# A decode attention block: most K and V loads issued by GpSimd as software DMAs, eight rows to a packet

## The chip, the cores and the metric

The kernel runs on one core of one Trainium2 chip. The metric is device time in microseconds for one execution. Three runs of the kernel before gave 1303.33, 1303.16 and 1303.37 us; the median is 1303.33 us. A separate execution was taken by the hardware profiler, and every row shown below comes from it.

## The reference

One decode step for two sequences (B = 2, one new token each, model width D = 512). It normalises x, projects it to one query for each of 32 heads of 128 channels, attends over a cache of 8192 positions, projects back, and then runs a channel MLP of width 1792. All numbers are float32.

```python
q = ((layernorm(x) @ wq).reshape(B, 1, 32, 128)).transpose(0, 2, 1, 3)
scores = einsum("bhqd,bhkd->bhqk", q, k_cache) * 128 ** -0.5
o = einsum("bhqk,bhkd->bhqd", softmax(scores), v_cache)
h = x + o.reshape(B, 1, 4096) @ wo
y = layernorm(layernorm(h))
out = h + gelu(y @ w1 + b1) @ w2 + b2
```

k_cache and v_cache are 2 x 32 x 8192 x 128 floats each: 268 MB each. Everything else together is about 24 MB. Each cache element is used once.

## The kernel before, in words

**Units.** The work is cut into 32 units. Unit i = 2g + b is a pair of heads (2g and 2g + 1) of sequence b. A unit's keys are 8.39 MB, and so are its values. One load puts such a block on 128 partitions, 64 partitions to a head, so that each partition receives one contiguous row of 64 KB: 128 positions of 128 channels. Sixteen DMA engines share the 128 rows, eight rows each.

**Slots.** SBUF has room for three such blocks, the three `kv` slots. `load` (L407) puts keys into slot 0 or 1 in turn (`i % 2`), and values into slot 2. So a load of values can start only when the previous values were used up, and a load of keys only when the keys of two units earlier were. Slot 2 first holds wq; after the last units, slot 0 takes wo and then w1, w2 and the biases, and slot 1 takes the last unit's values. The last values are loaded in two parts of 96 and 32 positions, and the very first keys in two halves.

**One unit.** VectorE multiplies the keys with the query (`multiply`, L441) in two chunks of 80 and 48 positions. GpSimd adds the upper 64 channels of the first chunk's products to the lower 64 (`halve`, L445), one instruction a unit (three in unit 0, which has four chunks of 32). VectorE sums over channels (`add_up`, L449) and takes the maximum (`row_max`, L456). After the second unit of a pair the maximum over partitions, the exponentials on ScalarE (L473) and the sum follow. TensorE multiplies the probabilities of unit i - 2 with its values (`values`, L485) while unit i's keys are worked on.

**The order of issue.** Instructions are written out by hand, and each engine runs its own in the order written. In the loop (L535 to L574), iteration i first issues the load of V[i - 2] (for i = 1 that is V[0], and none at i = 2), then that of K[i + 1], then the multiplies and the `halve` of unit i, then `values(i - 2)`. All these loads are issued by SyncE (SP), and SP has no other work, so its queue holds loads alone. A load waits on SP until its slot is free: for V on TensorE's `values`, for K on VectorE's `row_max`. `Waits` (L36) works out the semaphore waits of every instruction from the areas it reads and writes. `own` names a semaphore of its own for a load, so that it can be counted apart from the 16 shared ones.

**Behind the loop** (L577 on) the order written is: wo (SP, L419); a gather of 64 more rows of it into `wgt`, an indirect DMA of GpSimd's (L420), the one software DMA of the kernel before; V[30] (L578, SP); the head outputs and their projection (`project_all`, which needs wo and `wgt`); `values(30)`; V[31] in its two parts (L586, SP); biases, w1 and w2 (SP), which need the place where wo lay; then 24 matmuls that only keep TensorE's clock up (`keep_warm`), `values(31)`, the output projection's rest and the MLP. TensorE waits for the last piece of w2, adds it up, and the result is stored (L712).

Of the kernel before, what the change touches and what calls it, by code (L numbers as in the profile page):

```python
# [16 lines left out]
SHORT = (32, 32, 32, 32)  # L17
NG = 4
TH = 2
FILL = (24, 1, 4, 2, 3)  # L20
SR = 4
LW = 6
# [13 lines left out]
class Waits:  # L36
# [76 lines left out]
    def place(self, eng, op, areas):  # L113
        areas = [(x, w) for x, w in areas if x is not None]
        queue = (eng,)
        if "DMA" in op:
            kind = "soft" if eng == "Pool" else "hard"
            proc = kind, self.lane.get(kind, 0) % self.LANES
            if kind == "hard" and self.own:
                proc = self.own  # L120
            else:
                self.lane[kind] = self.lane.get(kind, 0) + 1
        else:
            proc = queue
        self.sem(proc)
        need = {}
        if proc != queue and self.count[proc]:
            need[proc] = self.count[proc]
        for (name, parts, cols), writes in areas:
            for r in self.mem.get(name, ()):  # L130
                if not (writes or r[4]) or not (r[2] & parts and r[3] & cols):
                    continue
                if r[0] == proc == queue:
                    if eng == "PE" or eng != "Pool" and not r[4]:
                        continue
                need[r[0]] = max(need.get(r[0], 0), r[1])
        clock = self.clock.setdefault(queue, {})
        todo = []
        for p, t in sorted(need.items(), key=lambda x: -self.after[x[0], x[1]][0]):
            if clock.get(p, 0) >= t:  # L140
                continue
            todo.append((p, t))
            for q, u in self.after[p, t][1].items():
                clock[q] = max(clock.get(q, 0), u)
        tick = self.count[proc] + 1
        if op != "Ldweights":
            self.count[proc] = tick
            self.after[proc, tick] = (len(self.after), {**clock, proc: tick})
        for (name, parts, cols), writes in areas:
            held = self.mem.setdefault(name, [])  # L150
            if writes:
                held[:] = [r for r in held if r[2] & ~parts or r[3] & ~cols]
            else:
                held[:] = [r for r in held if r[4] or r[0] != proc or r[2] & ~parts or r[3] & ~cols]
            held.append((proc, tick, parts, cols, writes))
        return proc, todo[::-1]
# [108 lines left out]
def tile_decode_block(nc, waits, x, k, v, wq, wo, wog, w1, bias, w2, out):  # L265
    B, H, SK, DH = k.shape
# [23 lines left out]
    def slot(at):  # L290
        return kv.tile([P, ROW], F32, name="kv", tag="kv", at=at)
# [22 lines left out]
    nc.gpsimd.memset(lt4, 0.0)  # L314
    oall = const.tile([P, H - TH, B], F32, name="oall")
    og = const.tile([P, SR, B], F32, name="og")
# [90 lines left out]
    def load(src, i, parts):  # L407
        g, b = units[i]
        t = slot(i % 2 if src is k or i == NU - 1 else 2)
        rows = src[b, 2 * g:2 * g + 2].rearrange("h (p j) d -> (h p) (j d)", j=NS2)  # L410
        waits.own = ("v" if src is v else "k", b) if len(parts) == 1 else None
        for s0, n in parts:
            nc.sync.dma_start(t[:, s0 * DH:(s0 + n) * DH], rows[:, s0 * DH:(s0 + n) * DH])
        waits.own = None
        return t

# [68 lines left out]
    def values(i, t):  # L485
        g, b = units[i]
        so, nu, w = so2[g == GL], NS2 // 4, 16
        for u in range(nu):
            n = u % NG
            if i == NU - 1 and u == 0:  # L490
                keep_warm(FILL[0])
            pe.matmul(so[32 * n:32 * n + w], ptz[b][:, u, :], t[:, u * 512:(u + 1) * 512],
# [26 lines left out]
    def project_all(wot):  # L519
        so = so2[0]  # L520
        parts = [(oall[:, h, :], wot[:, h, :]) for h in range(GA)]
        parts += [(og[:, r, :], wgt[:, r, :]) for r in range(SR)]
        parts += [(oall[:, h, :], wot[:, h - 2, :]) for h in range(GA + 2, H - TH)]
        n = len(parts)
# [7 lines left out]
    full = [(0, NS2)]  # L532
    assert NS2 == sum(LONG) == sum(SHORT)
    KT, VT = {0: load(k, 0, [(0, NS2 // 2), (NS2 // 2, NS2 // 2)])}, {}
    for i, (g, b) in enumerate(units):  # L535
        if i == 1 or i >= 3:
            j = max(i - 2, 0)
            VT[j] = load(v, j, full)
        if i + 1 < NU:
            KT[i + 1] = load(k, i + 1, full)  # L540
# [64 lines left out]
    def cut(parts, n):  # L605
        at[0] += n
        return late[:parts, at[0] - n:at[0]]

    zeros = cut(P, (TH + 1) * 32)
    nc.gpsimd.memset(zeros, 0.0)  # L610
    otz = zeros[:, :TH * 32].rearrange("p (s m) -> p s m", s=TH)
    lane = zeros[:B, TH * 32:]
    nc.gpsimd.tensor_copy(lane[:, 0:B], ident[:B, :B])
# [4 lines left out]

    wl = wot[:, H - 2 - TH:, :]
    wsum = const.tile([P, TH], F32, name="wsum")  # L620
# [20 lines left out]
    def keep_warm(n):  # L641
        for _ in range(n):
            pe.matmul(wp, wb[:, :P], wb, start=True, stop=True)
# [9 lines left out]
    def spread(row):  # L653
        return row.rearrange("d (n j c) -> d n c j", n=NG, c=DC)
# [8 lines left out]
    nc.vector.tensor_copy(b1t, b1p)  # L663
    keep_warm(FILL[1])
    for s in range(TH):
        for n in range(NG):
            pe.matmul(pc[32 * n:32 * n + 32], otz[:, s], spread(wlc[:, s])[:, n], start=False, stop=(s == TH - 1))
    keep_warm(FILL[2])
    cen = cut(P, DC * 32)
# [11 lines left out]
    for s in range(TH):  # L681
        for n in range(NG):
            pe.matmul(po2[32 * n:32 * n + 32], otz[:, s], wl[:, s, n * P:(n + 1) * P], start=False, stop=False)
    keep_warm(FILL[3])
    FH = FN // 2
# [10 lines left out]
    nc.scalar.activation(junk[:, 1:2], std, AF.Gelu_apprx_tanh)  # L696
    keep_warm(FILL[4])

# [67 lines left out]
```

## Time and profile before

| What | us |
|---|---|
| median of three runs | 1303.33 |
| the profiled execution, its own time | 1303.13 |
| the profiled execution's span | 1301.3 |
| VectorE busy | 973.6 (75%) |
| TensorE matmul busy | 385.9 (30%) |
| GpSimd busy | 364.6 (28%) |
| DMA queue q1 (SP's loads): share of 16 engines' span | 99.6% |

The span runs from the first to the last instruction of the profile; the execution's own time is 1.8 us longer. In the rows, `SPq` marks a DMA at the time when SP issues it; the transfer itself runs later. `kv<-in_k_dram` is a load of keys, `kv<-in_v_dram` one of values. In a timeline row the columns are start, length, engine, line, operation, tiles, shapes, count, and in brackets the idle time of the engine before it and what ended it. In a row of the chain the columns are start, length and what it was.

### The profile page before, as it was taken

The page shows a single profiled execution, that of the slowest core. Times are in us where ns is not written, and L with a number is a line of the kernel's source. Part 1 is how long each engine was busy: PE and PEld are TensorE (multiplying, and loading weights), DVE is VectorE, ACT ScalarE, POOL GpSimd, SP SyncE. Part 2 cuts the span into 40 slices and gives each one's busy share as a digit, 9 for nine tenths or more (in the row PEclk, how much of TensorE's full clock was granted, in tenths as well). Part 3 has the DMA queues.
Part 4 walks back from the last instruction along what each step waited for, and adds up shares of the span by engine and source line. Part 5 has one row for each costly group of instructions (what it writes and reads, how often), then busy time and mean ns, then how long its engine had stood idle before and what let it go on. Part 6 is the DMA issues. An engine that isn't in the chain of part 4 may idle for free.

```text
span 1301.3 us, 6275 instructions
## 1 busy us (share of the span) xinstructions
PE 385.9 (30%) x2756; PEld 118.2 (9%) x2756; DVE 973.6 (75%) x284; ACT 49.1 (4%) x156; POOL 364.6 (28%) x64
## 2 busy tenths in 40 slices
PE   3002322213332122333203232212323212332369
PEld 0000100101010010101001010000101001010113
DVE  1989989777779777779877778877778977777911
ACT  0000000000000000000000000000000000000011
POOL 1433333311333321233321233331133331133300
PEclk9556665566666556666556666556666556666569
DMA  9999999999999999999999999999999999999998
GB/s 403 435 451 420 447 421 445 425 429 439 423 447 423 445 422 447 423 437 433 425 443 425 443 423 447 421 441 429 433 437 423 445 423 447 421 445 425 438 422 373
DMA packets 10821, 561.13 MB, mean 431 GB/s; under 512 B 1398, under 2 KB 1398, under 8 KB 1660
## 3 DMA queue, kind: packets, MB, share of 16 engines
q1 hardware_dynamic: 10664, 560.48, 99.6%
q0 software_dynamic: 144, 0.52, 0.1%
q8 instruction: 5, 0.08, 0.0%
q14 instruction: 4, 0.03, 0.0%
q10 hardware_dynamic: 4, 0.00, 0.0%
HBM read 561.53 MB, written 0.00 MB: 432 GB/s over the span
## 4 chain that ended last, share of the span: by engine, by line
DMA 57%; DVE 37%; issue 2%; POOL 2%; PE 1%; SPq 0%; POOLq 0%
DMA kv<-in_k_dram 50%; DVE kv L441 22%; DVE s L449 15%; DMA kv<-in_w_dram 3%; POOL kv L445 2%; DMA wgt<-in_wog_dram,gidx 2%; DMA kv<-in_wq_dram 2%; PE so L188 1%; DVE qs L395 0%; DVE oall L507 0%; PE qps L188 0%; DVE rl L482 0%; PE sm L236 0%; SPq L598 0%; DVE q L385 0%
## 5 line engine op out<-in xcount | busy, mean ns | idle before, releaser
L441 DVE TENSOR_TENSOR kv<-kv,qps 128x10240 f32<-128x10240 f32 (+1 forms) x66 | 554.5, 8423 | 206.3 <-DMA kv<-in_k_dram 205.8
L445 POOL TENSOR_TENSOR kv<-kv 128x5120 f32<-128x5120 f32 (+1 forms) x34 | 356.0, 10470 | 864.8 <-DVE kv L441 864.8
L236 PE MATMUL so<-kv,pt 128*16 128x512 f32 x1920 | 273.6, 734 | 708.4 <-DMA kv<-in_v_dram 708.4
L449 DVE TENSOR_REDUCE s<-kv 128x48 f32<-128x6144 f32 (+1 forms) x66 | 381.5, 5820 | 1.4 <-POOL kv L445 0.3
L236 PEld LDWEIGHTS so<-kv,pt 128*16 128x16 f32 x1920 | 57.6, 113 | 901.1 <-DMA kv<-in_v_dram 712.6
L497 ACT ACTIVATE ss<-so 128x512 f32<-128x512 f32 x16 | 9.6, 597 | 1062.1 <-PE so L236 1047.8
L473 ACT ACTIVATE pt<-s,nb 64x128 f32<-64x128 f32 x64 | 25.5, 399 | 141.8 <-DVE nb L468 140.5
L236 PE MATMUL sm<-ident,mx 128*1 128x128 f32 x30 | 8.8, 293 | 57.3 <-DVE mx L456 57.3
L461 DVE TENSOR_REDUCE gm<-sm 1x4 f32<-1x256 f32 x16 | 6.6, 412 | 25.5 <-PE sm L236 25.0
L236 PE MATMUL sm<-sel,ss 128*128 128x4 f32 x120 | 15.8, 255 | 12.1 <-ACT ss L497 12.1
L236 PE MATMUL sm<-lt,ones 128*128 128x4 f32 x30 | 8.8, 365 | 34.9 <-ACT pt L473 34.9
L188 PE MATMUL qps<-kv,pt 128*16 128x512 f32 x128 | 16.7, 683 | 6.1 <-DMA kv<-in_v_dram 6.1
L236 PEld LDWEIGHTS sm<-sel,ss 128*128 128x128 f32 x120 | 14.5, 191 | 25.9 <-ACT ss L497 25.9
L385 DVE COPY q<-so 128x512 f32<-128x512 f32 x1 | 0.7, 691 | 20.8 <-PE so L188 20.8
L626 DVE TENSOR_SCALAR kv<-kv,wmean 128x512 f32<-128x512 f32 x2 | 1.0, 518 | 20.3 <-PE qps L188 20.3
L507 DVE TENSOR_TENSOR kv<-sm,rl 128x4 f32<-128x4 f32 x1 | 0.2, 163 | 19.3 <-PE sm L188 19.3
L188 PE MATMUL qps<-kv 128*32 128x128 f32 (+2 forms) x178 | 13.3, 296 | 0.6 <-DMA kv<-in_w_dram 0.6
L188 PE MATMUL so<-kv,yT 128*4 128x512 f32 x64 | 9.9, 787 | 11.5 <-DMA kv<-in_wq_dram 11.5
L188 PE MATMUL sm<-ident,mx 128*1 128x128 f32 x2 | 0.7, 371 | 40.2 <-DVE mx L456 40.2
L473 ACT ACTIVATION_READ_ACCUMULATOR pt<-s,nb 64x1 f32 x64 | 11.8, 184 | 0.0
L236 PE MATMUL qps<-qs,pick 4*128 4x128 f32 x60 | 11.1, 307 | 0.0
L236 PEld LDWEIGHTS sm<-lt,ones 128*128 128x128 f32 x30 | 7.5, 311 | 36.2 <-ACT pt L473 36.2
(108 smaller groups left out, 119.9 us busy)
## 6 DMA issues: line engine op xcount, KB each, us to landing
kv<-in_k_dram SPq DMA_DIRECT2D x2, 4096.0 KB, 35.7
kv<-in_wo_dram SPq DMA_DIRECT2D x1, 7680.0 KB, 46.3
kv<-in_v_dram SPq DMA_DIRECT2D x1, 6144.0 KB, 42.1
kv<-in_w_dram SPq DMA_DIRECT2D x1, 3584.0 KB, 34.3
kv<-in_v_dram SPq DMA_DIRECT2D x1, 2048.0 KB, 46.5
kv<-in_w_dram SPq DMA_DIRECT2D x1, 1792.0 KB, 38.2
kv<-in_w_dram SPq DMA_DIRECT2D x1, 1024.0 KB, 40.2
kv<-in_w_dram SPq DMA_DIRECT2D x1, 512.0 KB, 41.0
```

The costliest lines, as they stand in the source:

```text
L188: getattr(self.nc.tensor, what)(*aps, **how)
L236: ins = getattr(pe, what)(*aps, **how)
L385: nc.vector.tensor_copy(q2, so2[0])
L441: nc.vector.tensor_tensor(kc, kc, QP[g][:, b, None, :].to_broadcast([P, chunks(i)[c], DH]), op=ALU.mult)
L445: nc.gpsimd.tensor_tensor(kc[:, :, 0:HP], kc[:, :, 0:HP], kc[:, :, HP:DH], op=ALU.add)
L449: nc.vector.tensor_reduce(S[i][:, a:z], chunk(i, c, t)[:, :, 0:n], axis=AX.X, op=ALU.add)
L461: nc.vector.tensor_reduce(gm, MT.pop(g).rearrange("o b (s p) -> o b s p", s=2), axis=AX.X, op=ALU.max, negate=True)
L473: nc.scalar.activation(ptz[b][q, :, 4 * m:4 * m + 4], s[q], AF.Exp, bias=nb[q, b, e:e + 1], scale=SCALE, accum_out=lt4[q, m:m + 1])
L497: nc.scalar.activation(SS[g], so2[g == GL], AF.Copy)
L507: nc.vector.tensor_tensor(to, *(x.rearrange("p (b s) -> p s b", b=B) for x in (OP.pop(g), RL.pop(g))), op=ALU.mult)
L626: nc.vector.tensor_scalar(wlc[:, s], wl[:, s], wmean[:, s:s + 1], None, op0=ALU.subtract)
```

## The change

`load` chooses the issuing engine. Loads made in one part go to GpSimd's queue as software DMAs, except K[0] and K[1]; so do V[0] to V[30] and K[2] to K[31], 61 loads. K[0], K[1] and the two parts of V[31] stay on SP, and so do wq, wo, w1, w2 and the biases. [...] The place of each load in the written order is the same, but it now stands in GpSimd's order, among its `halve` instructions, and not in SP's. Its waits are the same. `own` now holds for software loads too.

```diff
+JOIN = True
 ...
             kind = "soft" if eng == "Pool" else "hard"
             proc = kind, self.lane.get(kind, 0) % self.LANES
-            if kind == "hard" and self.own:
+            if self.own:
                 proc = self.own
 ...
         rows = src[b, 2 * g:2 * g + 2].rearrange("h (p j) d -> (h p) (j d)", j=NS2)
-        waits.own = ("v" if src is v else "k", b) if len(parts) == 1 else None
+        soft = len(parts) == 1 and (src is v or i > 1)
+        queue = nc.gpsimd if soft else nc.sync
+        waits.own = ("v" if src is v else "k", b) if soft else None
         for s0, n in parts:
-            nc.sync.dma_start(t[:, s0 * DH:(s0 + n) * DH], rows[:, s0 * DH:(s0 + n) * DH])
+            queue.dma_start(t[:, s0 * DH:(s0 + n) * DH], rows[:, s0 * DH:(s0 + n) * DH], single_packet=soft and JOIN)
         waits.own = None
```

## The prediction

> **What bounds the kernel now.** I read the page's shares first, then the chain of waits, then the timelines of single engines around three places: the middle, the start and the end.
>
> ```profile
> span 1301.3 us, 6275 instructions
> PE 385.9 (30%) x2756; PEld 118.2 (9%) x2756; DVE 973.6 (75%) x284; ACT 49.1 (4%) x156; POOL 364.6 (28%) x64
> q1 hardware_dynamic: 10664, 560.48, 99.6%
> q0 software_dynamic: 144, 0.52, 0.1%
> ...
> 421.73 47.51 DMA kv<-in_k_dram
> 499.14 47.50 DMA kv<-in_k_dram
> ```
>
> SP's loads keep all 16 DMA engines busy for 99.6% of the span; no other engine comes near. The two chain pieces are the same step one pair of units later: 499.14 - 421.73 = 77.41 us for four loads of 8.39 MB, so 19.35 us a load and 2.42 us for each of the eight 64 KB rows that an engine moves of it. The kernel is a queue of transfers that must never run dry. Any idle time of the DMA engines is added to the end, and nothing but faster transfers can take time away.
>
> **The middle: no cost for the moved issue.** These are the timelines of SP, GpSimd and VectorE over one pair.
>
> ```profile
> 419.87 0.33 SPq L413 DMA_DIRECT2D kv<-in_v_dram  x1
> ...
> 402.75 11.04 POOL L445 TENSOR_TENSOR kv<-kv 128x5120 f32<-128x5120 f32 x1 [27.67 <-DVE kv L441]
> 441.47 11.04 POOL L445 TENSOR_TENSOR kv<-kv 128x5120 f32<-128x5120 f32 x1 [27.68 <-DVE kv L441]
> ...
> 430.56 17.29 DVE L441 TENSOR_TENSOR kv<-kv,qps 128x10240 f32<-128x10240 f32 x2 [8.54 <-DMA kv<-in_k_dram]
> ```
>
> The load of V goes out at 419.87, when `values` has freed slot 2; the load of K follows at 421.73, where the chain's piece begins. At that time the previous K is still in flight: VectorE gets it at 430.56. So V has 10.7 us before the DMA engines run dry. On GpSimd the written order is V, K, `halve`. The earlier `halve` is over at 413.79 and the next has its operand only at 441.4, so GpSimd sits idle where both issues now fall. What is queued behind them there is that next `halve`, and behind it VectorE's sum; both come 20 us later. Issue on GpSimd costs nothing here, as long as a software load is ready within 10.7 us. Taking the waits from SP gains nothing either.
>
> **What a software load needs to get ready.** Before has one software DMA, the gather of `wgt` behind the loop. The first two rows are queue totals between 1190 and 1260 us, the third comes from the table of DMA issues (last number: us to landing), the last two from GpSimd's timeline.
>
> ```profile
> q1 hardware_dynamic: 516, 29.98, 99.0%
> q0 software_dynamic: 144, 0.52, 1.9%
> ...
> wgt<-in_wog_dram,gidx POOLq DMA_INDIRECT x1, 25.3
> ...
> 1215.84 11.04 POOL L445 TENSOR_TENSOR kv<-kv 128x5120 f32<-128x5120 f32 x1 [27.66 <-DVE kv L441]
> 1227.06 1.24 POOL L420 DMA_INDIRECT wgt<-in_wog_dram,gidx  x1 [0.18 <-issue]
> ```
>
> It has 144 packets, nine an engine, of tiny size, yet lands after 25.3 us. That fits two queues taking turns packet by packet: each small packet waits for one large one of SP's. A partition's row of wo is 30 x 512 floats, 60 KB: 2.42 x 60/64 = 2.27 us; nine turns behind rows of 2.27 to 2.42 us are 21.0 us. The rest, 4.3 us, is the estimate from issue to ready, indices included; GpSimd is held 1.24 us of it. The shortest that any row shows is the final store, below, 1.4 us from issue to landing. I take 3 us for a plain load, bounds 1.4 and 4.3.
>
> **The start: one gap.** GpSimd, SP, TensorE, and the chain:
>
> ```profile
> 49.95 4.52 POOL L445 TENSOR_TENSOR kv<-kv 128x2048 f32<-128x2048 f32 x1 [2.25 <-DVE kv L441]
> 110.99 11.03 POOL L445 TENSOR_TENSOR kv<-kv 128x5120 f32<-128x5120 f32 x1 [25.91 <-DVE kv L441]
> 140.75 11.13 POOL L445 TENSOR_TENSOR kv<-kv 128x5120 f32<-128x5120 f32 x1 [18.73 <-DVE kv L441]
> ...
> 105.81 0.33 SPq L413 DMA_DIRECT2D kv<-in_v_dram  x1
> ...
> 140.26 9.15 PE L236 MATMUL so<-kv,pt 128*16 128x512 f32 x64 [9.88 <-DMA kv<-in_v_dram]
> ...
> 62.95 37.12 DMA kv<-in_k_dram
> ```
>
> K[2] lands at 62.95 + 37.12 = 100.07, so K[3] behind it at 119.42, and V[1] must be ready by then. SP issued it at 105.81. On GpSimd it stands behind unit 2's `halve`, which waits for K[2] and its multiply and runs from 110.99 to 122.02. V[1] is ready at 122.02 + 3 = 125.0: the DMA engines idle for **5.6 us** (4.0 to 6.9). Elsewhere the lead holds: V[0] stands behind unit 0's last `halve`, ready at 54.47 + 3 = 57.5, while K[1] occupies the engines until 100.07 - 2 x 19.35 = 61.4 (even 4.3 us fits). V[2] stands behind the `halve` that ends at 151.88, and behind `values(1)`, now over at 125.0 + 19.35 + 9.15 = 153.5; ready at 156.5, before K[4] lands at 163.7. From V[3] on `values` is the later of the two, as in the middle.
>
> **The end: V[30] is overtaken.** TensorE's timeline, SP's, and the issue table:
>
> ```profile
> 1224.30 9.84 PE L236 MATMUL so<-kv,pt 128*16 128x512 f32 x64 [27.58 <-DMA kv<-in_v_dram]
> 1262.21 9.66 PE L188 MATMUL qps<-kv,pt 128*16 128x512 f32 x64 [6.06 <-DMA kv<-in_v_dram]
> 1271.80 5.35 PE L188 MATMUL qps<-kv 128*128 128x512 bf16 x24
> 1277.08 7.06 PE L188 MATMUL qps<-kv,pt 128*16 128x512 f32 x64
> 1297.01 1.08 PE L188 MATMUL qps<-kv 128*32 128x128 f32 x32 [0.43 <-DMA kv<-in_w_dram]
> 1298.26 1.07 PE L188 MATMUL qps<-kv 128*32 128x128 f32 x24 [0.17 <-DMA kv<-in_w_dram]
> ...
> 1196.11 0.33 SPq L419 DMA_DIRECT2D kv<-in_wo_dram  x1
> 1234.29 1.28 SPq L413 DMA_DIRECT2D kv<-in_v_dram  x3
> ...
> out_dram<-kv SPq DMA_DIRECT2D x1, 4.0 KB, 1.4
> ```
>
> In SP's one queue the order was K[31], V[29], wo, V[30], V[31] in two parts, w1, w2. Now wo and V[31] are in SP's queue, and K[31], V[29], the gather, V[30] in GpSimd's. [...] V[30], behind the gather in its queue, starts after about four rows of V[31]'s first part, each 2.42 x 48/64 = 1.81 us: **7.2 us** late (three to five rows: 5.4 to 9.1). [...]
>
> Behind V[30] TensorE has no gap: `values(30)` at 1262.21, the 24 fillers, `values(31)`, end at 1284.14, with V[31] long there. From there to the end it waits for w2 only twice, 0.43 + 0.17 us. So of the 7.2 us **6.6 us** reach the end; the cover that is gone is the MLP's, which now lies behind the last transfer and not under it.
>
> **The joined packet.** Per MB, SP's packets cost 99.0 / 29.98 = 3.30% of that 70 us stretch; 0.52 MB would be 1.72%. The software ones took 1.9%; 0.18% of 16 x 70 us over 144 packets is 14 ns a packet (an estimate, rounded inputs). If all of it belongs to the packet and none to the row, joining saves seven of eight: 98 ns a load, 61 loads, 6.0 us. If all belongs to the row, nothing. No row decides; I take the middle, **-3.0 us**. A loss would need a gap between one load and the next; the next is queued 10 us early, so I leave that to a rival. [...]
>
> **Sum.** 5.6 + 6.6 - 3.0 = 9.2 us on 1303.13, the profiled execution's own time, is 1312.3; the median lies 0.2 above it: **1312.5 us**. Its own range, with the bounds (4.0 + 4.8 - 6.0 to 6.9 + 8.5 - 0): 1306 to 1319.
>
> **The rivals.**
>
> - *V[30] is not overtaken*, because the queues' turns are not even or the gather ends earlier. For it: nothing but the gather's 25.3 us speaks for even turns. Then 5.6 - 3.0: 1306 us.
> - *The rows are not joined in fact, and turns go row by row.* wo's rows then alternate with V[29]'s: V[29] arrives some 18 us late (eight rows of 2.27), V[30] is issued near 1252 and shares with the rest of V[31]: V[30] about 20 us late, and no saving: 1303.3 + 5.6 + 19.4 = 1328.
> - *A software load takes longer than 10.7 us to get ready.* Then every V opens a gap; at 15 us, 4.3 x 29 = 125 us: about 1430. The gather's 4.3 us speaks against it.
> - *Not slower: the packets' saving outweighs the gap.* Place: each of the 61 loads. It decides from 5.6 us on if V[30] is not overtaken, from 12.2 us if it is. At the top of the rounding, 18 ns a packet, it is 7.7 us: 1303.3 + 5.6 - 7.7 = 1301.2. Against it: this needs the upper end and no loss behind the loop.
>
> **How the numbers follow.** Forecast 0.54; not overtaken 0.19; row by row 0.09; slow software loads 0.04; not slower 0.14. A measurement of this kernel can tell 0.2%, 2.6 us, from no change. Of the last case 0.11 is faster and 0.03 within the bound; of the second 0.04 is within and 0.01 faster. So faster 0.12, same 0.07, slower 0.81. The range, 1300 to 1328, holds the first two cases, most of the last, and reaches the row-by-row case.
>
> **What would show it.** Gap: V[1] issued by GpSimd at 122.0, TensorE's second `values` starting at 145 and not 140.3, and DMA GB/s lower in the fourth of the 40 slices. Overtaking: `values(30)` more than 10 us later than 1262.2, TensorE no longer waiting for w2 at the end. Joined packets: q0 with far fewer than 61 x 144 packets, and the pair's step below 77.41 us (77.21 for 3.0 us in all). It is wrong if the second `values` starts by 141, or if the step shrinks by over 0.4 us.

## The result, and the profile after

The changed kernel takes **1325.63 us** (1325.46 to 1325.77, three runs) against 1303.33 us: a ratio of 1.0171, 95% interval 1.0148 to 1.0194, 22.3 us slower. Its profiled execution has a span of 1324.4 us and a time of 1325.77 us.

Four rows of the page of the kernel after. They correspond to the span, the engine shares and the two queue totals shown of before.

```profile
span 1324.4 us, 6275 instructions
PE 387.7 (29%) x2756; PEld 119.1 (9%) x2756; DVE 973.7 (74%) x284; ACT 49.1 (4%) x156; POOL 397.8 (30%) x125
...
q0 software_dynamic: 8928, 512.23, 89.5%
q1 hardware_dynamic: 1880, 48.77, 8.6%
```

No engine does more, apart from GpSimd: 33 us more in 61 more instructions, the issues. The loads have moved to q0. Its packets are 8928, and that is 61 x 144 + 144: as many for each load as a load with a packet a row has (128 rows of 65,536 B and 16 short ones), the other 144 being the gather's. In the records, then, nothing is joined, although these loads ask for a single packet (`single_packet` in the diff; "the flag" from here on). The kernel without the flag (experiment 1) has the same 8928, so the count alone cannot tell whether the flag joins rows; the order in which they are served, below, says more.

**The start.** GpSimd's timeline of the kernel after, then TensorE's, then a piece of the chain (line numbers are higher by 1 to 3 than before):

```profile
111.16 11.03 POOL L448 TENSOR_TENSOR kv<-kv 128x5120 f32<-128x5120 f32 x1 [14.65 <-DVE rl L485]
122.12 0.56 POOL L416 DMA_DIRECT2D kv<-in_v_dram  x1
...
144.47 8.60 PE L237 MATMUL so<-kv,pt 128*16 128x512 f32 x64 [13.94 <-DMA kv<-in_v_dram]
...
122.12 22.30 DMA kv<-in_v_dram
```

V[1] goes out the moment unit 2's `halve` ends, at 122.12, and `values(1)` starts at 144.47, where it started at 140.26 before. Of the 22.30 us from issue to landing 19.35 are the transfer; 2.95 us lie before, in and behind it. By the packet records of the trace no row of a load starts between 118.3 and 123.4 us; V[1]'s first rows start at 123.41, 1.3 us after the issue, and take 3.19 us where a row otherwise takes 2.42.

**The middle.** GpSimd's timeline and the chain, 400 to 500 us, kernel after:

```profile
408.67 11.04 POOL L448 TENSOR_TENSOR kv<-kv 128x5120 f32<-128x5120 f32 x1 [19.35 <-DVE rl L485]
426.55 0.56 POOL L416 DMA_DIRECT2D kv<-in_v_dram  x1 [6.85 <-PE so L237]
427.93 0.54 POOL L416 DMA_DIRECT2D kv<-in_k_dram  x1 [0.81 <-DVE mx L459]
447.37 11.04 POOL L448 TENSOR_TENSOR kv<-kv 128x5120 f32<-128x5120 f32 x1 [18.91 <-DVE kv L444]
...
417.14 8.93 PE so L237 x64
494.54 9.48 PE so L237 x64
```

Both issues fall where GpSimd was idle. From one pair to the next `values` moves by 494.54 - 417.14 = 77.40 us; before it was 77.41.

**The end.** VectorE's timeline, TensorE's, SP's and GpSimd's of the kernel after, the queue totals between 1206 and 1240 us, then those of four short stretches in turn (from 1222.2, 1224.5, 1226.9 and 1229.2 us, 1.4 us each; a row counts whole where it starts, hence the shares above 100%), and q1's between 1247 and 1262 us:

```profile
1217.40 17.29 DVE L444 TENSOR_TENSOR kv<-kv,qps 128x10240 f32<-128x10240 f32 x2 [15.33 <-DMA kv<-in_k_dram]
...
1248.12 9.73 PE L237 MATMUL so<-kv,pt 128*16 128x512 f32 x64 [45.72 <-DMA kv<-in_v_dram]
1287.38 8.88 PE L189 MATMUL qps<-kv,pt 128*16 128x512 f32 x64 [10.56 <-DMA kv<-in_v_dram]
1296.19 5.35 PE L189 MATMUL qps<-kv 128*128 128x512 bf16 x24
1301.47 7.06 PE L189 MATMUL qps<-kv,pt 128*16 128x512 f32 x64
1318.48 4.02 PE L189 MATMUL qps<-kv 128*128 128x512 bf16 x115
...
1201.78 0.33 SPq L422 DMA_DIRECT2D kv<-in_wo_dram  x1
1246.70 0.94 SPq L416 DMA_DIRECT2D kv<-in_v_dram  x2
...
1258.27 0.59 POOL L416 DMA_DIRECT2D kv<-in_v_dram  x1 [17.72 <-PE so L237]
...
q1 hardware_dynamic: 125, 7.68, 52.2%
q0 software_dynamic: 128, 7.34, 49.9%
...
q1 hardware_dynamic: 15, 0.92, 152.0%
q0 software_dynamic: 15, 0.98, 162.1%
q1 hardware_dynamic: 15, 0.92, 152.1%
q0 software_dynamic: 15, 0.98, 162.3%
...
q1 hardware_dynamic: 128, 6.29, 99.8%
```

While wo (q1) and K[31] or V[29] (q0) are both waiting, the engines serve 125 rows of the one (7.68 MB at 61,440 B) and 112 of the other (7.34 MB at 65,536 B; the other 16 packets of q0 are of 4 B and took turns of their own, so its 128 stand against 125). The four short stretches hold a row of wo, a row of V[29], a row of wo, a row of V[29] on 15 of the 16 engines: they take turns row by row, the load with the flag too. VectorE waits 15.33 us for K[31], and V[29] is there at 1248.12 and not at 1224.30. V[30] cannot be issued before `values(29)` is through, 1258.27, and meanwhile the first part of V[31], on SP since 1246.70, goes through whole (128 rows, 6.29 MB); the rows of its second part take turns with those of V[30]. `values(30)` starts at 1287.38, 25.2 us later than before. Behind it TensorE has no gap, and its last group no longer waits for w2: it is the work behind V[30] that sets the end, not the last transfer. TensorE's granted clock is 1.00 from the 24 fillers to the end (1296 to 1324 us here, 1272 to 1300 before) and 0.61 between 200 and 1180 us in both kernels; that the fillers keep it up was not tried apart.

### The profile page after: what moved, and what is told of

Same layout as the page of the kernel before. It is cut to its first block, busy times and chain, and to the rows that moved or that the text cites. A ratio compares the mean times of both kernels' runs of the same rounds, so it can differ in the third digit from the quotient of the medians.

```text
span 1324.4 us, 6275 instructions
## 1 busy us (share of the span) xinstructions
PE 387.7 (29%) x2756; PEld 119.1 (9%) x2756; DVE 973.7 (74%) x284; ACT 49.1 (4%) x156; POOL 397.8 (30%) x125
## 3 DMA queue, kind: packets, MB, share of 16 engines
q0 software_dynamic: 8928, 512.23, 89.5%
## 4 chain that ended last, share of the span: by engine, by line
DMA 71%; PE 24%; DVE 3%; POOL 1%; issue 1%
DMA kv<-in_v_dram 66%; PE so L237 21%; DMA kv<-in_k_dram 3%; PE qps L189 2%; DVE kv L444 2%; DMA kv<-in_wq_dram 2%; POOL kv L448 1%; PE so L189 1%; DVE s L452 1%; PE sm L189 0%; PE rowacc L189 0%; DVE q L386 0%; DVE kv L677 0%; DVE kv L673 0%; DVE kv L714 0%
## 5 line engine op out<-in xcount | busy, mean ns | idle before, releaser
L237 PE MATMUL so<-kv,pt 128*16 128x512 f32 x1920 | 277.3, 743 | 736.0 <-DMA kv<-in_v_dram 736.0
L416 POOL DMA_DIRECT2D kv<-in_v_dram x31 | 17.7, 570 | 214.2 <-PE so L237 214.2
L416 POOL DMA_DIRECT2D kv<-in_k_dram x30 | 16.1, 538 | 36.0 <-DVE s L452 22.9
L629 DVE TENSOR_SCALAR kv<-kv,wmean 128x512 f32<-128x512 f32 x2 | 0.9, 517 | 22.3 <-PE qps L189 22.3
L386 DVE COPY q<-so 128x512 f32<-128x512 f32 x1 | 0.7, 691 | 20.4 <-PE so L189 20.4
```

The lines of the kernel that those rows point to most:

```text
L237: ins = getattr(pe, what)(*aps, **how)
L386: nc.vector.tensor_copy(q2, so2[0])
L416: queue.dma_start(t[:, s0 * DH:(s0 + n) * DH], rows[:, s0 * DH:(s0 + n) * DH], single_packet=soft and JOIN)
L629: nc.vector.tensor_scalar(wlc[:, s], wl[:, s], wmean[:, s:s + 1], None, op0=ALU.subtract)
```

## The experiments

All times are medians; ratios are to runs of the kernel before on the same chip (medians 1303.18 to 1303.30 us). Of the longer edits the lines that matter are shown; `...` marks what is left out.

**1. Without joining.**

```diff
-JOIN = True
+JOIN = False
```

> The changed kernel with JOIN = False, nothing else. Theory A (the eight rows asked for as one packet are still served row by row, and joining saves no time): 1325.6 us, within 1.3 us (0.1%); wo's rows and those of V[29] alternate one by one as they do with joining, and the step of a pair stays at 77.41 us. Rival B (joining saves part of a packet's cost on 61 loads): slower, by up to 3 us, about 1328.6, step of a pair up by 0.2 us.

1325.34 us, ratio 1.0169 (1.0152 to 1.0186), against 1.0171 with joining. The queue totals between 1206 and 1240 us of this kernel:

```profile
q0 software_dynamic: 129, 7.41, 50.3%
q1 hardware_dynamic: 115, 7.00, 47.6%
```

The same turns: 114 rows of wo (7.00 MB) and 113 of V[29] and K[31] (7.41 MB). `values(28)` starts at 1190.63 us here and at 1191.27 with joining, so the step of a pair is the same within 0.1 us. Asking for one packet changed neither the order nor the time. A is right, B falls.

**2. The gap at the start taken away.** Unit 2 without its `halve`; VectorE sums all channels of that chunk.

```diff
-            if c < nch - 1:
+            if c < nch - 1 and i != 2:
                 halve(i, c, kt)
...
-            add_up(i, 0, kt, HP)
+            add_up(i, 0, kt, HP if i != 2 else DH)
```

> The changed kernel, but unit 2 has no halve on GpSimd: VectorE sums all 128 channels of that chunk (5.3 us more of VectorE there). V[1] no longer stands behind it. Theory A (the 5.7 us by which every later load is late come from V[1] standing behind that halve, and nothing takes them up later): V[1] issued near 109 us, no idle stretch of the DMA engines at 119, end 5.7 us earlier: about 1320. Rival B (the end hangs on the turns behind the loop alone and the gap is taken up there): 1325.6, unchanged.

1321.97 us, ratio 1.0143 (1.0126 to 1.0160): 3.7 us earlier. GpSimd's timeline of this kernel:

```profile
109.34 0.54 POOL L416 DMA_DIRECT2D kv<-in_v_dram  x1 [12.95 <-PE so L237]
...
146.13 11.06 POOL L448 TENSOR_TENSOR kv<-kv 128x5120 f32<-128x5120 f32 x1 [10.31 <-DVE kv L444]
157.14 0.56 POOL L416 DMA_DIRECT2D kv<-in_v_dram  x1
```

V[1] now goes out at 109.34, and the gap at 119 is gone. A's number, 1320, is missed by 2 us: the gap was smaller than 5.7 us (experiment 7), and unit 2's longer sums on VectorE (17.28 us for the two, 11.95 in other units) push unit 3's `halve` back, and V[2] stands behind that until 157.14. `values(2)` then starts 39.75 us behind `values(1)` (180.15 - 140.40), where before it was 38.71 (178.97 - 140.26): a new gap of 1.0 us. B (unchanged) falls.

**3. One queue behind the loop.** wo, V[31], the biases, w1 and w2 issued by GpSimd as well, wo ahead of the last `halve`. `load_wo_rows` is the load of wo taken out of `load_wo`, which keeps the gather.

```diff
-        queue = nc.gpsimd if soft else nc.sync
+        queue = nc.gpsimd if soft or i == NU - 1 else nc.sync
...
             KT[i + 1] = load(k, i + 1, full)
+        else:
+            wot = load_wo_rows(nc.gpsimd)
...
-    nc.sync.dma_start(br[0::P // NG], bias)
+    nc.gpsimd.dma_start(br[0::P // NG], bias)
-    nc.sync.dma_start(w1t, w1v)
+    nc.gpsimd.dma_start(w1t, w1v)
-        nc.sync.dma_start(w2t[:, t:t + n, :], w2v[:, t:t + n, :])
+        nc.gpsimd.dma_start(w2t[:, t:t + n, :], w2v[:, t:t + n, :])
```

> The changed kernel, but wo, the two parts of V[31], the biases, w1 and w2 are issued by GpSimd too, wo ahead of the last halve, so that behind the start there is one queue, in the order of the kernel before. Theory A (the loss behind the loop is the taking of turns between two queues): V[29] lands 5.7 us later than in the kernel before (1230), values(30) starts near 1268, TensorE waits for w2 at the end again; only the gap at the start is left: about 1309. Rival B (the loss is in the software loads themselves, or in issuing V[30] behind GpSimd's work): stays above 1320.

1316.03 us, ratio 1.0098 (1.0081 to 1.0115): 9.6 us earlier than the changed kernel, 7 us later than A's number. B (above 1320) falls, and A's number is not met. The next run, with the same edit behind the loop, shows why.

**4. Both edits.**

> Both edits at once: no halve in unit 2, and one queue behind the loop. Theory A (the two losses are separate and are all there is; joining saves nothing): 1303.3 us, the time of the kernel before, within 1.5 us. Rival B (joining does save up to 3 us, hidden in the changed kernel by other losses): 1300.5. Rival C (a software load costs the DMA queue something each time): 0.1 us a load would be 1309.

1312.76 us, ratio 1.0072 (1.0055 to 1.0089). It is 9.5 us off A's number. GpSimd's and TensorE's timelines of this kernel behind the loop:

```profile
1254.52 1.06 POOL L605 DMA_DIRECT2D kv<-in_w_dram  x2
1264.59 0.53 POOL L605 DMA_DIRECT2D kv<-in_w_dram  x1 [9.02 <-issue]
1279.63 0.54 POOL L605 DMA_DIRECT2D kv<-in_w_dram  x1 [14.50 <-issue]
...
1225.31 9.39 PE L237 MATMUL so<-kv,pt 128*16 128x512 f32 x64 [27.58 <-DMA kv<-in_v_dram]
1264.33 8.65 PE L189 MATMUL qps<-kv,pt 128*16 128x512 f32 x64 [10.20 <-DMA kv<-in_v_dram]
1281.51 6.89 PE L189 MATMUL qps<-kv 128*128 128x512 bf16 x24 [8.52 <-POOL kv L643]
```

V[29] and V[30] are nearly back in place: 1225.31 and 1264.33, where before had 1224.30 and 1262.21. What is new is my edit's own: the third and fourth load of w2 held GpSimd for 9.02 and 14.50 us, and behind them stood the memset that TensorE's fillers need. TensorE waited 8.52 us for it.

**5 and 6. Why GpSimd was held.** One kernel writes the loads of w1 and w2 behind that memset; the other only doubles `dynamic_dma_scratch_size`.

```diff
     nc.gpsimd.memset(wb, 0.0)
+    nc.gpsimd.dma_start(w1t, w1v)
+    for t, n in ((0, 7), (7, 4), (11, 2), (13, 1)):
+        nc.gpsimd.dma_start(w2t[:, t:t + n, :], w2v[:, t:t + n, :])
```

> The kernel with both edits (no halve in unit 2; one queue behind the loop), and the loads of w1 and w2 written behind GpSimd's last memset. In the kernel with both edits two of w2's four loads held GpSimd for 9.0 and 14.5 us, and the memset that TensorE's fillers wait for stood behind them. Theory A (that hold is the whole rest, 8.5 us; the turns and the first gap are the only losses of the change): values(30) near 1263, no wait of TensorE on that memset, about 1304.5 (1.2 us stay, since V[2] now stands behind unit 3's halve). Rival C (software loads cost the queue something of their own): stays above 1308.

```diff
-                     dynamic_dma_scratch_size=1024)
+                     dynamic_dma_scratch_size=2048)
```

> The kernel with both edits, and the space for software descriptors raised from 1024 to 2048 bytes a partition; w1 and w2 where they were. [...]

1304.55 and 1304.53 us, both with the ratio 1.0011 (1.0002 to 1.0021, and 1.0001 to 1.0020). With 2048 the four loads of w2 leave in one go; GpSimd's timeline of that kernel:

```profile
1253.96 0.56 POOL L601 DMA_DIRECT2D kv<-in_w_dram  x1
1254.52 2.10 POOL L605 DMA_DIRECT2D kv<-in_w_dram  x4
```

So it was this setting that held GpSimd: 9.02 and 14.50 us at 1024, no hold at 2048. Had it been anything else, the 1312.76 us of the kernel with both edits would have stayed. In the kernel with w1 and w2 written late the last load of w2 is still held, for 8.55 us, but nothing stands behind it. With the hold out of the way, 70 software loads in SP's place cost 1.3 us in all (the 61, and wo, V[31], the biases, w1 and w2). The small gap at V[2] belongs to the first of the two edits (in the kernel with both, `values(2)` starts at 179.61, 0.6 us later than before); that it is the whole of the 1.3 us was not tried apart. C, which asked for more than 1308, falls.

**7. The gap alone.** As 5, but with unit 2's `halve` in place.

> The changed kernel with one queue behind the loop and w1 and w2 written late, but with unit 2's halve in place: the gap at the start alone. Theory A: V[29] lands 4.5 us later than in the kernel with both edits, about 1309.0. Rival (the gap is taken up where the end is bound by the queue again): 1304.5.

1307.98 us, ratio 1.0039 (1.0023 to 1.0054): the rival (1304.5) falls, and the time is 1.0 us below A's number. The gap is worth 1307.98 - 1303.18 = **4.8 us** at most, since this kernel too has 70 software loads and what they cost of their own is in it. The rest of the change, 1325.63 - 1307.98 = **17.6 us**, is the loss behind the loop.

**8. No joining, one queue.** As 5, with `JOIN = False`.

> The kernel with both edits and w1 and w2 written late, without joining. Theory A (joining saves nothing, with no second queue about either): 1304.5 us, within 0.7. Rival B (joining saves part of a packet's cost): up to 3 us slower.

1304.71 us, ratio 1.0011 (1.0002 to 1.0020), against 1304.55 us with joining. Joining saves nothing that can be measured here: the medians lie 0.16 us apart, and single runs of one and the same kernel differ by 0.7 us here and by 1.5 us there.

**9 and 10. Half the mending.** First wo alone in GpSimd's queue, then V[31] alone; the edits are those lines of 3.

> The changed kernel with wo alone moved to GpSimd's queue, ahead of the last halve; V[31], w1 and w2 stay on SP. Turns row by row: V[29] no longer shares, lands near 1230, and V[30] is issued at 1240. But V[31]'s rows, on SP from 1240 too, now alternate with wo's last rows, the gather's nine turns and V[30]'s rows, and V[30] lands near 1285: about 1323. Rival (the loss is wo's alone): 1309.

> The changed kernel with the two parts of V[31] alone moved to GpSimd's queue, behind V[30]; wo, w1 and w2 stay on SP. Turns row by row: V[29] still shares with wo and lands at 1248; V[30] is issued at 1258 and the DMA engines have nothing between 1247 and 1261; then w1 and w2 on SP alternate with V[31]'s rows, and V[31] lands late: about 1331, slower than the changed kernel. Rival (the loss is that V[31] overtakes V[30]): 1309.

1327.84 us, ratio 1.0190 (1.0173 to 1.0207), and 1333.78 us, ratio 1.0228 (1.0211 to 1.0245). Neither half alone helps: wo alone is 2.2 us slower than the changed kernel (the two intervals overlap), V[31] alone 8.2 us. Both rivals (1309) fall. TensorE's timelines, first two rows of wo alone, then four of V[31] alone:

```profile
1229.11 9.68 PE L237 MATMUL so<-kv,pt 128*16 128x512 f32 x64 [27.57 <-DMA kv<-in_v_dram]
1289.05 8.73 PE L189 MATMUL qps<-kv,pt 128*16 128x512 f32 x64 [18.92 <-DMA kv<-in_v_dram]
```

```profile
1247.55 9.72 PE L237 MATMUL so<-kv,pt 128*16 128x512 f32 x64 [45.75 <-DMA kv<-in_v_dram]
1279.86 8.76 PE L189 MATMUL qps<-kv,pt 128*16 128x512 f32 x64 [3.62 <-DMA kv<-in_v_dram]
1304.19 7.00 PE L189 MATMUL qps<-kv,pt 128*16 128x512 f32 x48 [10.29 <-DMA kv<-in_v_dram]
1313.38 2.67 PE L189 MATMUL qps<-kv,pt 128*16 128x512 f32 x16 [2.19 <-DMA kv<-in_v_dram]
```

With wo moved V[29] is on time (1229.11), but V[31] is issued on SP at 1239.02, and V[30] is there only at 1289.05. I had 1285, so the expectation was 4 us low. With V[31] moved the DMA engines have almost nothing to do from 1247 to 1259 us (a share of 0.07), as was expected, and V[30] is at 1279.86; but then `values(31)` waits for V[31] twice, 10.29 and 2.19 us, with w1 and w2 on SP. The time is 2.8 us above the expected 1331. Both times lie near those worked out from turns row by row (1323 and 1331); the rows of these two kernels were not counted.

**11. Two hardware queues.** The kernel before with one edit: wo issued by ScalarE, ahead of the last `halve`.

```diff
+        else:
+            wot = load_wo_rows(nc.scalar)
```

> The kernel before, no software load of K or V, but wo issued by ScalarE (a second hardware queue) ahead of the last halve. Theory A (turns row by row belong to any two queues, not to software loads): wo alternates with K[31] and V[29], V[29] lands near 1242, V[30] waits on SP for values(29) until about 1252 with V[31] behind it, and the DMA engines have nothing for some 12 us: about 1315. Rival (the turns are a matter of the software queue): 1303.3.

1315.51 us, ratio 1.0097 (1.0082 to 1.0112). Queue totals of this kernel between 1206 and 1235 us, and TensorE's timeline:

```profile
q1 hardware_dynamic: 114, 6.49, 51.8%
q10 hardware_dynamic: 102, 6.08, 48.5%
...
1242.41 8.58 PE L236 MATMUL so<-kv,pt 128*16 128x512 f32 x64 [45.76 <-DMA kv<-in_v_dram]
```

Half and half again, 99 rows each (6.49 MB at 65,536 B, 6.08 MB at 61,440 B; the rest are short), and V[29] at 1242.41, 18 us late. V[30] waits on SP for `values(29)`, which runs until 1250.99, with V[31] behind it: SP's four issues, V[29] to V[31], end at 1252.42. A's number is met and the rival (1303.3) falls. These two hardware queues took turns too, so the turns do not need a software load.

## Why the prediction was right or wrong

The direction was right and the size was not: 9.2 us forecast, 22.3 measured. Two terms of the sum failed: the 7.2 us by which V[30] was to come late, 6.6 of them at the end, and the 3.0 us that joining was to save. **Both take the eight rows that a DMA engine moves of a load for one packet**, served in one go, so that V[29] would be nearly in time. That was my assumption, from the meaning of the words; nothing in before was joined, and no run shows it. The runs showed in its place that the rows of a load are served in turn with the other queue's, row by row, with the flag (125 rows of wo to 112) or without it (114 to 113). The 6.6 us were 17.6, and the 3.0 us were nothing. Whether the flag joins no rows, or the engines take turns within a joined packet, no run tells apart; the title's eight rows to a packet are not borne out by the records, 8928 packets with the flag and without it.

- *The middle.* Right: `halve` and issues do not meet, the lead of 10.7 us is enough (V[1]'s first rows start 1.3 us after its issue), and nothing is gained from SP's side.
- *Ready after 3 us.* Too long. V[1] was to be ready at 125.0, and its first rows start at 123.41, 1.3 us after the issue and not 3. The 2.95 us between issue and landing beside the transfer are near 3 by luck; they are not the time to get ready.
- *The gap at V[1].* Right in place and mechanism: 5.6 us forecast, 4.8 us at most measured by the run with the gap alone. The 3 us were the term that was too big.
- *V[30] overtaken.* The term of 6.6 us was really 17.6. The cause given, about four rows of V[31] ahead of it, is not what happened. wo alternated with K[31] and V[29] from the first row on; V[29] was 19.0 us late beyond the gap (1248.12 - 1224.30 - 4.8). V[30] was issued so late that V[31]'s first part went ahead whole and its second took turns with it; of the 20.4 us by which V[30] came late beyond the gap, 17.6 reach the end. That the end is then set by TensorE's work behind V[30], and that the wait for w2 goes, was right.
- *The joined packet.* -3.0 us forecast, nothing measured, twice (1325.34 against 1325.63 us, 1304.71 against 1304.55). Whether the 14 ns a packet are real no run shows; asking for one packet took none of it away.
- *The rivals.* "The rows are not joined in fact, and turns go row by row" had V[29] 18 us late, V[30] about 20 us late and 1328 us; measured were 19.0 us, 1287.38 - 1262.21 - 4.8 = 20.4 us, and 1325.6 us. It was worked out nearly to the number and given 0.09. The rows that it rests on were quoted: the gather's 25.3 us fit small packets that wait behind one row each, not behind loads. What I missed is that the gather speaks for turns between rows and gives no reason to believe in longer ones.

What stays open beside that: whether the flag is without effect for rows of 64 KB only. Smaller rows were not tried. No version tried beats the kernel before; the nearest is 1.3 us behind it.

## What to carry to other kernels

A load's place in the queue is part of the schedule. Here one queue's order let the next buffer free up in time. With wo in another queue, wo landed no earlier (1242.7 us, 1242.4 before), and V[29], which overlapped it, was there at 1248.12 in place of 1224.30. So move all of a stretch or none (all behind the loop: 1307.98 us; some: 1325.63, 1327.84 and 1333.78), and look first at the loads whose landing releases the next issue. And a load that moves to an engine with work of its own inherits that work's place in order: find the one place where the instruction ahead of it ends later than the wait it had before.

## What the runs showed of the hardware

- Where two DMA queues had rows waiting, each got every other row (125 rows to 112, and 16 short packets, in 34 us, hardware and software; 99 to 99 in 29 us, two hardware queues), also where a software load asked for a single packet. The trace records the rows singly; whether the engine, too, takes each for a packet no run shows.
- A software load of 128 rows held GpSimd for 0.56 us. On idle DMA engines V[1]'s first rows started 1.3 us after the issue, and issue to landing was 2.95 us more than the 19.35 us of the transfer. 70 loads issued by GpSimd in place of SP's cost 1.3 us in all (1304.55 against 1303.23 us).
- With `dynamic_dma_scratch_size` at 1024, and V[30], V[31], the biases, w1 and two loads of w2 issued just before, the next two loads held GpSimd, and everything written behind them, for 9.02 and 14.50 us; with 2048 there was no hold, and 8.2 us came back (1312.76 to 1304.53 us).
